# Both halves of the last batch's mix behind the branch to the general path

## The chip, the cores and the metric

One core of a Trainium2 chip runs the kernel. Its engines are TensorE (PE; PEld is its weight load), VectorE (DVE), ScalarE (ACT), GpSimd (POOL) and SyncE (SP), each with its own queue of instructions, released by semaphores. The metric is the device time of one execution in microseconds, median of 3 runs.

## The reference

Four batches of 6208 steps by 256 channels. A gated scan runs along the steps of each batch; then the 128 steps with the highest score (a dot product with `w_gate`) go through a small two-layer network and are mixed back into their rows of the output:

```python
f = lower_bound + (1 - lower_bound) * sigmoid(f_logit);  i = 1 - f
for t in range(S):
    h = f[:, t] * h + i[:, t] * x[:, t];  y[:, t] = h
scores = y @ w_gate
for b in range(B):
    top = argpartition(-scores[b], 128)[:128]
    xe = y[b, top]
    ye = relu(xe @ w1) @ w2                      # 256 -> 1024 -> 256
    out[b, top] = y[b, top] + sigmoid(scores[b, top])[:, None] * ye
```

## The kernel before, in words

The steps are cut into 29 units (`UNITS`), 7 or 8 per batch. For each unit SP loads `ft` and `xt`; ACT makes the gates, POOL and DVE the inputs, DVE scans, PE takes scores and turns the tiles, ACT (and DVE for some) copies them to `ym`, and SP stores them to `out`. After a batch's last unit `choose(b)` finds its 128 rows with a fast search (`idx` and `aim`, the row numbers), and counts in `tally` (DVE, line 480) whether that search could be trusted.

Then `experts(b)` works on these rows: POOL fetches them from `out` (indirect DMA, line 529) into `xe`; PE turns them, and ACT and DVE copy them to `xT`; DVE takes the gate's product (`ask`, line 559), ACT its sigmoid (`opened`, line 563); PE multiplies by `w1` (`up`, 570 or 579), ACT applies the relu (587), PE multiplies by `w2` (`down`, 592 or 597) into PSUM; DVE mixes the product with the row (`mix`, 601 or 604) into `res`; POOL scatters `res` back to `out` (indirect DMA, line 608).

For the last batch, b = 3, `down` and `mix` are cut into two halves of 128 channels (`down_half`, `mix_half`). Both halves of `down` write the one PSUM tile `acc`, columns 0 to 127 and 128 to 255; each is 8 products, which the trace shows as 16 records, so 32 on line 597 in all. `mix_half` is

```python
v.scalar_tensor_tensor(st["res"][:, c], st["py"][:, c], st["open"], st["xe"][:, c], ALU.mult, ALU.add)
```

The **general path** is for inputs on which the fast search fails in some batch. It is an unrolled exact search for all batches (some 7,200 instructions in POOL's queue, few in the others'), and stands behind a branch:

```python
def redo_all():
    v.tensor_reduce(total, tally[:1], AX.X, ALU.add)                    # line 716, DVE
    val = nc.values_load(total[0:1, 0:1], engines=ENGINES)             # line 717: POOL, PE, ACT, DVE
    with tc.If(val != 0):                                              # line 718
        for b in range(B):
            redo(b)
```

DVE adds up `tally`; then POOL, PE, ACT and DVE each load the sum into a register (TENSOR_LOAD) and each branch on it (COMPARE_BRANCH). With these inputs the sum is zero and every engine jumps over the general path to the join behind it. On POOL, the join and the last scatter are all that is left.

The order in each engine's queue comes from a planner, the class `Plan`: each step is put in with `add(engine, cost, emit, rank, after, key)`; the planner simulates the engines with these costs, takes among ready steps the one with the lowest rank, and emits the code in the order of its start times. `after` are the keys that must have been started in its simulation before a step is. Semaphore waits are then derived from the order of emission: a write into `acc` that is emitted after a read of `acc` waits for it, whichever columns they use. The branch is the step `("redo",)`, emitted after the last `down` of batch 3. Line 790 is the end of the program, where the engines meet.

Of the kernel before, what the change touches and what calls it, by code (L numbers as in the profile page):

```python
# [22 lines left out]
NF = F // P  # L23
# [36 lines left out]
class Plan:  # L60
# [6 lines left out]
    def add(self, engine, cost, emit, rank, after, key=None, late=0.0, takes=(), load=1.0):  # L67
        if key is not None:
            self.at[key] = len(self.ops)
        self.ops.append((engine, cost, emit, rank, [k for k in after if k is not None], late, takes, load * cost))  # L70
# [110 lines left out]
def gated_scan_moe(tc, xin, fin, lbwg, w1, w2, outs, cap):  # L181
    nc = tc.nc
    v, a, pe, g = nc.vector, nc.scalar, nc.tensor, nc.gpsimd
    with ExitStack() as ctx:
# [57 lines left out]
        add = plan.add  # L242
# [371 lines left out]
        def experts(b):  # L614
            st = {}
            fetch, turn_in, take, ask, opened, up, relu, down, mix, scatter = stages(b, st)
            turn_half, take_half, up_half, down_half, mix_half, copy_indices, see = st["half"]
            halved = b == B - 1
            p0 = 20.0 * last_unit[b] + EXPERT[b]
            k = lambda *t: ("moe", b, *t)  # L620

            prev = ("mix", b - 1)
            if halved:
                add("pool", 0.15, copy_indices, p0, [("st", b)], ("index", b))
                for i in range(last_unit[b - 1] + 1, N - 1):
                    add("pool", 0.1, lambda i=i: see(i), p0, [("store", i), ("index", b), ("seen", i - 1)], ("seen", i))
            add("pool", 1.04, fetch, p0, [("st", b), ("index", b), ("seen", N - 2) if halved else None, ("store", last_unit[b])], k("fetch"))
            add("sw", 0.36, None, p0 - 1e3, [k("fetch")], k("xe"), late=LAND[b])
            plan.tile(("pm", b, 0), ("pt", "pt"), [("xT", b)])
            if halved:  # L630
                plan.tile(("pm", b, -1), ("pt", "pt"), [("xT", b, 1)])
                for h in range(NH):
                    add("pe", 0.18, lambda h=h: turn_half(h), p0 - 2, [k("xe"), ("moe", b - 1, "down", NF - 1), k("flip", h - 1)], k("flip", h), takes=[("pm", b, -h)])
                    add("dve" if h else "act", 0.28, lambda h=h: take_half(h), p0 - 2, [k("flip", h)], ("xT", b, h) if h else ("xT", b))
            else:
                add("pe", 0.36, turn_in, p0, [k("xe"), ("moe", b - 1, "down", NF - 1)], k("flip"), takes=[("pm", b, 0)])
                add("act", 0.38, take, p0 - 1, [k("flip")], ("xT", b))
            if b in ASKED:
                add("dve", 0.6, ask, p0, [k("xe"), prev, ("wgrow",)], k("ask"))
            else:  # L640
                add("pe", 0.3, ask, p0 - 1, [("xT", b), prev], k("ask"), load=0.1)
            add("act", 0.22, opened, p0 - 1, [k("ask")], k("open"))
            for f0 in range(0, NF, TP) if halved else ():
                for h in range(NH):
                    add("pe", 0.95, lambda f0=f0, h=h: up_half(f0, h), p0, [("xT", b, h) if h else ("xT", b), k("up", f0 - 1), k("uph", f0) if h else None],
                        k("up", f0 + TP - 1) if h else k("uph", f0), takes=[("pm", b, 1 + f0 // TP)])
            for f in range(0 if halved else NF):
                add("pe", 0.49, lambda f=f: up(f), p0, [("xT", b), k("up", f - 1)], k("up", f), takes=[("pm", b, 1 + f // TP)] if f % TP == 0 else [])
            for f0 in range(0, NF, TP):
                plan.tile(("pm", b, 1 + f0 // TP), ("pt", "pt"), [k("relu", f0)])  # L650
                add("act", 0.6, lambda f0=f0: relu(f0), p0 - 1, [k("up", f0 + TP - 1)], k("relu", f0))
            for h in range(NH if halved else 0):
                for f in range(NF):
                    add("pe", 0.24, lambda f=f, h=h: down_half(f, h), p0, [k("relu", f // TP * TP), k("up", NF - 1), k("downh", NF - 1) if h else None, k("down" if h else "downh", f - 1), k("ask"), ("flag", b)],
                        k("down" if h else "downh", f), load=1.0)
            for f in range(0 if halved else NF):
                add("pe", 0.46, lambda f=f: down(f), p0, [k("relu", f // TP * TP), k("up", NF - 1), k("down", f - 1), k("ask"), None if b in APART else ("flag", b),
                                                         ("forget", N - 1, 1) if b in APART else None], k("down", f), takes=[("py", b)] if b in APART else [], load=1.5)
            if b in APART:
                plan.tile(("py", b), ("gt", "gt"), [("mix", b)])  # L660
            if halved:
                add("dve", 0.33, lambda: mix_half(0), p0 - 1, [k("downh", NF - 1), k("open")], k("mixh"))
                add("dve", 0.33, lambda: mix_half(1), p0 - 1, [("redo",), k("mixh"), k("open")], ("mix", b))
            else:
                add("dve", 0.5, mix, p0 - 1, [k("down", NF - 1), k("open")], ("mix", b))
            add("pool", 1.04, scatter, p0, [("mix", b), ("flag", b), ("moe", B - 1, "fetch")], k("scatter"))
            add("sw", 0.36, None, p0 - 1e3, [k("scatter")], ("scatter", b), late=DONE)
# [88 lines left out]
        for b in range(B):  # L756
            choose(b)
            experts(b)
# [35 lines left out]
```

## Time and profile before

| | |
|---|---|
| runs | 212.99 us median of 3 (212.47 to 213.47) |
| the profiled execution | 212.7 us, of which the span from first to last instruction is 210.3 us |
| busy, share of the span | PE 74%, PEld 48%, DVE 75%, ACT 74%, POOL 76% |
| HBM | 53.48 MB read, 25.95 MB written, 378 GB/s over the span |
| granted TensorE clock | 0.905 over the span, 1.00 from 190 to 205 us |
| DMA share, 190 to 195 us; 195 to 200; 200 to 205; 205 to 210 | 0.17; 0.13; 0.02; 0.08 |

The page cuts the span into 40 slices of 5.26 us and gives the busy share of each engine, and of the core's 16 DMA engines, in tenths. The timeline lists instructions in order of time with their idle time before and what released them. The views of a line list its instructions, and those of an engine's sequencer with a q behind the engine's name (POOLq, DVEq, PEldq). The chain that ended last is followed back from the last instruction.

### The profile page before, as it was taken

Reading aid. Unit: us, or ns where it says so; the run is one execution under the profiler, and the core shown is the slowest. Engines: PE = TensorE matmul, PEld = TensorE weight load, DVE = VectorE, ACT = ScalarE, POOL = GpSimd, SP = SyncE. Lnnn points to the kernel's source line nnn. Section 1 sums busy time; section 2 is a strip of 40 time slices with the busy share of each in tenths; the row PEclk is TensorE's granted clock in tenths of the full one; section 3 lists DMA queues with packets and bytes.
Section 4 is the critical chain, followed back from the end, with each engine's and each line's share of the span. In section 5 each row is a group of like instructions: output and inputs, shape, how many; then the busy total and the mean of one; then the engine's idle time right before and its main releaser. Section 6 shows DMA issues by size and latency. Waiting matters only on the chain. (4 is left out here: it accounts for less than half of the span.)

```text
span 210.3 us, 3398 instructions
## 1 busy us (share of the span) xinstructions
PE 155.4 (74%) x1191; PEld 101.9 (48%) x1191; DVE 157.5 (75%) x200; ACT 155.6 (74%) x210; POOL 159.7 (76%) x162
## 2 busy tenths in 40 slices
PE   0775636677779576773878999895699899999950
PEld 0233424444345444431436786462397556467950
DVE  2389599998799998868598979998795988650110
ACT  4698989989869899799868969777988956241300
POOL 5389999784989999987999896597999997024301
PEclk9999999999655999998558999979599999999997
DMA  6999999999999999999999999999999999991100
GB/s 219 382 428 427 427 425 417 429 428 418 417 433 425 421 423 424 433 430 424 414 423 435 414 423 434 424 414 426 420 435 421 422 419 420 422 397 61 65 5 30
DMA packets 13684, 79.69 MB, mean 379 GB/s; under 512 B 1760, under 2 KB 2016, under 8 KB 5728
## 3 DMA queue, kind: packets, MB, share of 16 engines
q1 hardware_dynamic: 13136, 78.39, 89.4%
q0 software_dynamic: 384, 1.05, 1.3%
q8 instruction: 11, 0.18, 0.3%
q14 instruction: 9, 0.07, 0.1%
q10 hardware_dynamic: 144, 0.00, 0.0%
HBM read 53.48 MB, written 25.95 MB: 378 GB/s over the span
## 5 line engine op out<-in xcount | busy, mean ns | idle before, releaser
L293 DVE TENSOR_TENSOR_SCAN xt<-gt,xt 128x1024 f32<-128x1024 f32 (+4 forms) x58 | 114.1, 1984 | 18.1 <-POOL xt L283 14.7
L283 POOL TENSOR_TENSOR xt<-xt,ft 128x1024 f32<-128x1024 f32 (+13 forms) x54 | 91.4, 1699 | 6.5 <-ACT ft L271 3.6
L309 PE MATMUL pt<-ident,xt 128*128 128x128 f32 x384 | 69.7, 323 | 5.0 <-ACT ym L326 3.0
L309 PEld LDWEIGHTS pt<-ident,xt 128*128 128x128 f32 x384 | 54.6, 202 | 30.6 <-ACT ym L326 13.8
L302 PE MATMUL score<-xt,wgr 128*32 128x256 f32 (+1 forms) x400 | 42.6, 439 | 35.5 <-DVE xt L293 34.8
L275 ACT ACTIVATE gt<-ft,nl 128x1024 f32<-128x1024 f32 (+4 forms) x58 | 56.9, 984 | 8.6 <-DVE xt L293 7.4
L279 POOL TENSOR_SCALAR xt<-xt,nl 128x1024 f32<-128x1024 f32 (+13 forms) x54 | 46.3, 861 | 15.4 <-DMA xt<-x 13.7
L326 ACT COPY ym<-pt 128x512 f32<-128x512 f32 (+1 forms) x93 | 48.6, 555 | 8.2 <-PE pt L309 7.8
L271 ACT ACTIVATE ft<-ft 128x2048 f32<-128x2048 f32 (+4 forms) x29 | 47.3, 1632 | 9.2 <-DMA ft<-fl 9.2
L302 PEld LDWEIGHTS score<-xt,wgr 128*32 128x32 f32 x400 | 9.7, 115 | 47.0 <-DVE xt L293 35.7
L290 DVE SCALAR_TENSOR_TENSOR xt<-gt,xt 128x640 f32<-128x640 f32 (+10 forms) x22 | 14.1, 641 | 2.4 <-ACT gt L275 2.4
L461 POOL TENSOR_SCALAR hot<-slot,rank 128x128 bf16<-128x128 bf16 x14 | 8.4, 605 | 9.3 <-DVE vals L456 7.6
L579 PE MATMUL pm<-xT,w1t 128*128 128x128 f32 x96 | 12.1, 280 | 0.4 <-ACT xT L550 0.4
L608 POOL DMA_INDIRECT out<-res,aim x4 | 4.0, 1000 | 10.9 <-issue 10.6
L579 PEld LDWEIGHTS pm<-xT,w1t 128*128 128x128 f32 x96 | 11.2, 192 | 1.3 <-ACT xT L550 0.9
L448 DVE TENSOR_SCALAR_CACHE_REDUCE junk<-acc,mine 128x448 bf16<-128x448 f32 x14 | 9.6, 682 | 2.0 <-ACT junks L445 1.3
L587 ACT ACTIVATE hT<-pm 128x512 f32<-128x512 f32 x8 | 4.8, 596 | 6.3 <-PE pm L570 2.6
L326 DVE COPY ym<-pt 128x512 f32<-128x512 f32 (+1 forms) x11 | 6.9, 627 | 2.2 <-PE pt L309 2.2
L592 PE MATMUL acc<-w2t,hT 128*128 128x256 f32 x32 | 7.3, 382 | 0.0
L592 PEld LDWEIGHTS acc<-w2t,hT 128*128 128x128 f32 x32 | 5.9, 190 | 1.1 <-issue 0.4
L601 DVE SCALAR_TENSOR_TENSOR res<-acc,open,xe 128x128 f32<-128x128 f32 x2 | 0.7, 349 | 7.5 <-PE acc L597 7.5
L529 POOL DMA_INDIRECT xe<-out,idx x4 | 4.6, 1143 | 2.0 <-issue 0.8
(99 smaller groups left out, 91.4 us busy)
## 6 DMA issues: line engine op xcount, KB each, us to landing
ft<-fl SPq DMA_DIRECT2D x20, 1024.0 KB, 16.0
xt<-x SPq DMA_DIRECT2D x20, 1024.0 KB, 15.5
out<-ym SPq DMA_DIRECT2D x20, 1024.0 KB, 15.1
ft<-fl SPq DMA_DIRECT2D x3, 832.0 KB, 15.5
xt<-x SPq DMA_DIRECT2D x3, 832.0 KB, 15.5
out<-ym SPq DMA_DIRECT2D x3, 768.0 KB, 17.5
out<-ym SPq DMA_DIRECT2D x5, 256.0 KB, 16.4
ft<-fl SPq DMA_DIRECT2D x4, 256.0 KB, 16.1
```

The source lines that it names most:

```text
L271: a.activation(fs[i], fs[i], ACTF.Sigmoid, scale=-1.0)
L275: a.activation(gs[i, h][:, :n], fs[i][:, h], ACTF.Identity, scale=nl[:, h : h + 1], bias=1.0)
L279: g.tensor_scalar(xs[i][:, h, c0:], xs[i][:, h, c0:], nl[:, h : h + 1], 1.0, ALU.mult, ALU.mult)
L283: g.tensor_tensor(xs[i][:, h, c0:], xs[i][:, h, c0:], fs[i][:, h, c0:], ALU.mult)
L290: v.scalar_tensor_tensor(xs[i][:, h, :c1], gs[i, h][:, :c1], 1.0, xs[i][:, h, :c1], ALU.subtract, ALU.mult)
L293: v.tensor_tensor_scan(xs[i][:, h], gs[i, h][:, :n], xs[i][:, h], carry[h] if blk0 else 0.0, ALU.mult, ALU.subtract)
L302: pe.matmul(score[j * CG : (j + 1) * CG, b % 2, c0:], wgr[:, h, CG - 1 - r : 2 * CG - 1 - r], xs[i][:, h, c + c0 : c + BLK], start=(h == 0 ...
L309: pe.transpose(pts[key][:, q * P : (q + 1) * P], xs[i][:, h, tail + c :: cols], ident)
L326: (v.tensor_copy if eng == "dve" else a.copy)(out, src)
L448: v.tensor_scalar(junk, acc[:, :ROW], st["mine"][:, k : k + 1], None, ALU.is_gt, ALU.add, accum_out=st["rank"][:, k : k + 1])
L579: pe.matmul(st["pm", f // TP][:, c : c + P], w1t[:, h, f * P : (f + 1) * P], st["xT"][:, h], start=(h == 0), stop=(h == NH - 1))
L592: pe.matmul(st["py"][:, :D], st["hT"][:, f], w2t[:, f], start=(f == 0), stop=(f == NF - 1))
```

## The change

One entry in the list of steps that the first half of the last mix must come after: the branch, `("redo",)`.

```diff
             if halved:
-                add("dve", 0.33, lambda: mix_half(0), p0 - 1, [k("downh", NF - 1), k("open")], k("mixh"))
+                add("dve", 0.33, lambda: mix_half(0), p0 - 1, [("redo",), k("downh", NF - 1), k("open")], k("mixh"))
                 add("dve", 0.33, lambda: mix_half(1), p0 - 1, [("redo",), k("mixh"), k("open")], ("mix", b))
```

On DVE, at the end of the program, before (line 601 is the mix of the last batch, 716 the sum of `tally`, 717 and 718 the load of the sum and the branch; lines 559 and 604 behind the branch belong to the general path):

```order
L543 COPY xT_1868<-pm 128x128 [waits PE_49]
L559 SCALAR_TENSOR_TENSOR res,gate<-xe_109,wgrow 128x256 [waits DMASW3_49]
L601 SCALAR_TENSOR_TENSOR res<-acc,open,xe_109 128x128 [waits PE_49,Activation_49]
L716 TENSOR_REDUCE total<-tally 1x1
L717 TENSOR_LOAD total [waits DVE_49]
L718 COMPARE_AND_BRANCH
...
L718 UNCONDITIONAL_BRANCH
L718 UNCONDITIONAL_BRANCH [waits DVE_49]
L601 SCALAR_TENSOR_TENSOR res<-acc,open,xe_109 128x128 [waits PE_49]
L790 UNCONDITIONAL_BRANCH
```

and now:

```order
L543 COPY xT_1868<-pm 128x128 [waits PE_49]
L559 SCALAR_TENSOR_TENSOR res,gate<-xe_109,wgrow 128x256 [waits DMASW3_49]
L716 TENSOR_REDUCE total<-tally 1x1 [waits DVE_49]
L717 TENSOR_LOAD total [waits DVE_49]
L718 COMPARE_AND_BRANCH
...
L718 UNCONDITIONAL_BRANCH
L718 UNCONDITIONAL_BRANCH [waits DVE_49]
L601 SCALAR_TENSOR_TENSOR res<-acc,open,xe_109 128x128 [waits PE_49,Activation_49]
L601 SCALAR_TENSOR_TENSOR res<-acc,open,xe_109 128x128
L790 UNCONDITIONAL_BRANCH
```

The sum of `tally` now stands right behind `ask` (line 559), with no wait for PE ahead of it; both mixes stand behind the join, the first with the waits for PE and ACT, the second with none.

On PE, at the second product of the second half of `down`:

```order
 L597 MATMUL acc<-w2t,hT 128x128 x3
 L597 MATMUL acc<-w2t,hT 128x128 [waits Activation_49]
-L597 MATMUL acc<-w2t,hT 128x128 x4
-L597 MATMUL acc<-w2t,hT 128x128 [waits DVE_49]
-L597 MATMUL acc<-w2t,hT 128x128 x6
+L597 MATMUL acc<-w2t,hT 128x128 x11
 L717 TENSOR_LOAD total [waits DVE_49]
 L718 COMPARE_AND_BRANCH
```

The ninth product is the first of the second half; the tenth waited for DVE (for the first mix, which reads `acc`), and now no product of the second half waits for DVE.

On POOL the order is the same in both. This is its end, ahead of the branch and behind the general path:

```order
L608 DMA out<-res,aim 6208x256 [waits DMASW2_49,DVE_49]
L717 TENSOR_LOAD total [waits DVE_49]
L718 COMPARE_AND_BRANCH
...
L718 ISA [waits Pool_49,DMASW4_49,DMASW5_49,DMASW3_49,DMASW6_49,DMASW2_49,DMASW7_49,DMASW1_49,DMASW0_49]
L718 UNCONDITIONAL_BRANCH
L608 DMA out<-res,aim 6208x256 [waits DMASW6_49,DMASW5_49,DMASW7_49,DMASW3_49,DVE_49]
L790 UNCONDITIONAL_BRANCH
```

POOL's load of the sum follows the scatter of batch 2 and waits for DVE's line 716; the last scatter waits for DVE (the mixes) and for DMAs.

## Rows read from the trace of the kernel before

**Rows 1.** The page's slices: mean busy share of the DMA engines, in tenths.
```profile
DMA  6999999999999999999999999999999999991100
```

**Rows 2.** Timeline, 180 us to the end: start, us, engine, line, what [idle before <-releaser].
```profile
194.16 0.48 DVE L604 SCALAR_TENSOR_TENSOR res<-py,open,xe 128x256 f32<-128x256 f32 x1 [5.17 <-PE py L592]
...
195.44 0.08 DVE L559 DVE_READ_ACCUMULATOR res<-xe,wgrow 128x1 f32 x1
195.50 0.98 POOL L608 DMA_INDIRECT out<-res,aim  x1 [0.30 <-DVE xT L543]
...
198.78 2.23 PE L597 MATMUL acc<-w2t,hT 128*128 128x128 f32 x18
198.98 0.60 ACT L587 ACTIVATE hT<-pm 128x512 f32<-128x512 f32 x1 [1.13 <-PE pm L570]
201.13 0.35 DVE L601 SCALAR_TENSOR_TENSOR res<-acc,open,xe 128x128 f32<-128x128 f32 x1 [5.61 <-PE acc L597]
201.39 0.13 DVE L716 TENSOR_REDUCE total<-tally 1x1 int32<-1x4 f32 x1
...
201.53 1.83 PE L597 MATMUL acc<-w2t,hT 128*128 128x128 f32 x14 [0.52 <-DVE total L716]
203.40 0.35 DVE L601 SCALAR_TENSOR_TENSOR res<-acc,open,xe 128x128 f32<-128x128 f32 x1 [1.87 <-PE acc L597]
206.51 0.98 POOL L608 DMA_INDIRECT out<-res,aim  x1 [10.03 <-issue]
```

**Rows 3.** Line 717, loads of the sum: ns min/median/max, first and last start us.
```profile
L717 POOLq TENSOR_LOAD <-total x1: 513/513/513, 201.6 to 201.6; - x1
...
L717 PEldq TENSOR_LOAD <-total x1: 493/493/493, 201.6 to 201.6; - x1
```

**Rows 4.** Line 718, the branches and what stands at the join.
```profile
L718 POOLq EVENT_SEMAPHORE  x5: 17/43/43, 204.8 to 205.1; - x5
...
L718 POOLq COMPARE_BRANCH  x1: 53/53/53, 202.1 to 202.1; - x1
L718 DVEq COMPARE_BRANCH  x1: 72/72/72, 202.2 to 202.2; - x1
L718 PEldq COMPARE_BRANCH  x1: 3577/3577/3577, 202.2 to 202.2; - x1
...
L718 DVEq EVENT_SEMAPHORE  x1: 21/21/21, 202.4 to 202.4; - x1
L718 POOLq INC_SWDGE_SEM  x1: 328/328/328, 205.2 to 205.2; - x1
L718 PEldq EVENT_SEMAPHORE  x1: 51/51/51, 205.8 to 205.8; - x1
```

**Rows 5.** DMA queues (packets, MB, share), 195 to 201.5 us; then 203 to 204.2.
```profile
q0 software_dynamic: 96, 0.26, 10.0%
...
q8 instruction: 1, 0.02, 6.0%
q14 instruction: 1, 0.01, 2.2%
```

**Rows 6.** The chain that ended last: start us, us, what.
```profile
204.77 0.09 issue
...
205.76 0.53 issue
206.29 1.21 POOLq L790
```

**Rows 7.** Line 790, the program's end, 204.5 to 206.4 us.
```profile
L790 PEldq DRAIN  x1: 8/8/8, 206.0 to 206.0; - x1
L790 POOLq DRAIN  x1: 2994/2994/2994, 206.3 to 206.3; - x1
```

**Rows 8.** Timeline again: POOL's fetch for batch 3, released by a transfer.
```profile
190.64 0.09 POOL L516 MEMSET ym<- 1x1 f32 x1 [2.32 <-DMA out<-ym]
191.45 1.11 POOL L529 DMA_INDIRECT xe<-out,idx  x1 [0.72 <-DMA out<-ym]
```

## The prediction

> **What bounds the kernel now.** I read the page's slices first: the DMA engines are at 90% or more up to the 36th of 40 slices, so up to about 190 us the kernel is a stream of loads and stores, and behind that it is a chain of small steps for the last batch [rows 1]. The change sits in that chain, so the second view is the timeline from 180 us on. The third is the chain that ended last, and the fourth the two lines of the branch, since the timeline leaves out what sequencers do.
>
> The timeline shows DVE's half of the story [rows 2]. The first mix starts at 201.13 us, 5.61 us after DVE's last step, once PE has done the first half of `down` and one product more. The sum of `tally` comes behind it, at 201.39, although it reads nothing that the mix writes: it is late only because it stands behind the mix in DVE's queue. PE sat idle for 0.52 us until DVE was through and went on at 201.53. The row names line 716 as the releaser, but by the order it is the mix that ends at 201.48 (PE writes `acc`, which the mix reads). PE's last product ends at 201.53 + 1.83 = 203.36, the second mix runs from 203.40 to 203.75, and the last scatter starts on POOL at 206.51, 2.76 us after `res` was whole.
>
> Those 2.76 us are the matter. The four engines load the sum at 201.6, in about 0.5 us [rows 3]. POOL branches at 202.1, in 53 ns, and then shows nothing until its first event at the join at 204.77 [rows 4, 6]: 204.77 - 202.15 = 2.62 us. In that gap the DMA queues carry one packet on each of the two instruction queues, where 195 to 201.5 us had only those of the software queue [rows 5]. I read it as POOL, which jumps over some 7,200 instructions, waiting for the code at its target. PE shows the same as a branch of 3577 ns; DVE is at its join 0.2 us after its branch [rows 4]. At 205.76 POOL is through the join, 3.61 us after its branch, and 0.75 us later the scatter starts [rows 6, 2]. So what ends last is: first mix, sum, load, branch, code, join, scatter. The second mix, at 203.75, is not on that path.
>
> **The change, step by step.**
>
> *The sum and the branch go forward.* The sum now follows `ask`, whose last record ends at 195.52 [rows 2]. With 0.13 us for itself it is done by about 195.7, instead of 201.52. POOL stands behind the scatter of batch 2, which ends at 196.48 [rows 2]. Whether its sequencer takes the load while that scatter runs, or behind it, no row tells: with 0.1 us to start and 0.51 us [rows 3], the branch ends between 196.4 and 197.2. Adding the 3.61 us from branch to the end of the join, POOL stands ready at the last scatter's wait between 200.0 and 200.8, over 2.5 us ahead of the mixes. Load, code and join thus cost nothing; what hides them is the second half of PE's work, and if the code took 2.5 us longer they would show again. The one transfer that the join may have to wait for, batch 2's scatter, is no later than before.
>
> *PE's wait goes.* No product of the second half waits for DVE now. 0.52 us go, and PE's last product ends at 203.36 - 0.52 = 202.84. Its input from ACT is done at 198.98 + 0.60 = 199.58, well before the fifth product needs to follow [rows 2], so nothing else is late there.
>
> *Both mixes come behind the last product.* The first starts 0.12 us after PE (201.01 to 201.13) or 0.04 us (203.36 to 203.40), by the two rows there are [rows 2]; the two take 0.35 us each, back to back. `res` is whole at 202.84 + 0.04 to 0.12 + 0.70 = 203.58 to 203.66; I take 203.62. That is 0.13 us earlier than 203.75: one mix more behind PE costs 0.35, the wait gives 0.52 back. DVE itself waits in the branch from 195.7 to about 196.6, when nothing else is queued for it.
>
> *The scatter now starts from `res`.* How long POOL takes from a release to its start I bound by three rows. The fetch of batch 3 started 0.72 us after the last small step ahead of it (190.73 to 191.45) [rows 8]; the last scatter itself 0.75 us after the join [rows 6, 2]; the scatter of batch 2 0.86 us after its mix ended at 194.64 [rows 2], where it also stood behind another scatter, so this is an upper bound. I take 0.79: 203.62 + 0.79 = 204.41, and 206.51 - 204.41 = 2.10 us are gained. The ends are 203.58 + 0.72 and 203.66 + 0.86, that is 2.21 and 1.99 us.
>
> *The end moves along.* From the scatter's start to the end of the span are 210.3 - 206.51 = 3.8 us: descriptors, landing and the engines' meeting, in which POOL's drain takes up 2.99 us, from 206.29 to 209.28 [rows 7]. Its cover is PE: PE came to the end at 206.0 [rows 7]. If PE reaches the load only when its products are done, it is there at 202.84 + 0.49 + 3.58 + 0.2 = 207.1, and POOL's drain would end at 209.28 - 2.10 = 207.18. So PE is in time even then, by little.
>
> Sum: 212.7 - 2.1 = 210.6 us against the profiled execution. That one is 0.29 us below the median of the runs, so I expect a median of 212.99 - 2.1 = **210.9 us**, 1.0% less.
>
> **A rule against it.** POOL's gap begins at its branch and holds a code packet [rows 4, 5], and I price that branch at 2.62 us. The Trainium skill (Advanced Engine Details and Errata, Control Flow Timing) gives about 108 ns for a compare-and-branch, by which an early branch would be worth next to nothing and only the mixes' 0.13 us would be left. The same skill (Runtime: NRT & Kernel Launch, Instruction fetch mechanics) says that a taken branch whose target is outside the two loaded pages waits for a DMA fetch. The rows bear out the first for POOL's and DVE's own records (53 and 72 ns), and the second for what follows on POOL and PE.
>
> **The rivals.**
>
> *No gain.* POOL's join is late for a cause other than its branch, one that stays, for instance that it follows `res`: 204.77 is 1.02 us after the second mix ended. Then only `res` moves, by 0.13 us, and the time is 212.9. For it: the profile names no releaser for that stretch, only "issue". Against it: by the order the join waits for POOL and DMAs and not for DVE, and the code packets. 8%.
>
> *Slower: the first mix is released by PE's join.* Standing behind the branch, it could be held until PE too has passed, whose event there came at 205.8, 3.58 us after its branch began [rows 4]. If PE takes the load only behind its last product, the join is at 202.84 + 0.1 + 0.49 + 3.58 = 207.0, `res` at 207.7, the scatter at 208.5: 2.0 us later, 215.0 us. If it takes the load as soon as its products are queued, near 199.7, the join is at 203.9 and it would still be a gain of 1.1 us. It decides at 206.51 - 0.79 - 0.70 = 205.0: a later join makes the kernel slower, which is a PE branch that begins after 201.4. Against it: the second mix stood behind the same join before and started 0.04 us after PE's last product, 2.4 us before PE's event. 5%.
>
> *More.* POOL has long been waiting when `res` comes, and starts as soon after it as one scatter follows another, 0.30 us [rows 2]: 203.92, a gain of 2.6 us, 210.4. For it: its sequencer has nothing left to do. Against it: the fetch of batch 3, whose sequencer had also waited, took 0.72. 10%, and within the range.
>
> **The numbers.** The forecast with its own ends has 77%, more gain 10%, no gain 8%, slower 5%. The run-to-run spread of the kernel before (212.47 to 213.47) is the largest part of the range: 210.4 less 0.3 is 210.1; 210.9 plus 0.1 for the ends plus 0.5 for the spread, and 0.3 for a code load that shows again in part, is 211.8. Of changes in time about 0.5%, or 1.07 us, can be told from none, so faster means under 211.93 us. That gives faster 86% (77 and 10, less 1 for a median that the spread lifts over the bound), the same 9%, slower 5%.
>
> **What would show it.** Right: the sum on line 716 near 195.6 us, POOL's branch near 197 and its join over by 201, a code packet near 198; line 597 on PE in one run of 32 records without idle time, ending near 202.8; the two mixes back to back from about 202.9; the last scatter near 204.4, released by DVE and not by "issue". Wrong: a last scatter that still starts over 2 us after the second mix, with events of POOL's join between them; a first mix that starts well behind PE's last product; or a PE that comes to the end after POOL's drain, which would take back part of the gain at line 790.

## The result and the profile after

The changed kernel takes 210.74 us in the median of 6 runs (209.70 to 211.79), the kernel before 213.0 us (212.47 to 214.10). The ratio is 0.9887 with a 95% interval of 0.9842 to 0.9932: faster by 1.4 to 3.4 us. A second measurement gave 0.9916 (0.9884 to 0.9948; 211.99 us median of 10 runs against 213.39). One run in the table of experiments, 212.78 us of the kernel "bank and order", counts as a slow run and is left out of that kernel's median, range and ratio. The profiled execution of the change took 209.75 us, its span 207.4 us.

The timeline of the changed kernel from 195 us on (start, us, engine, line, what, idle before and releaser) answers to [rows 2]:

```profile
195.39 0.08 DVE L559 DVE_READ_ACCUMULATOR res<-xe,wgrow 128x1 f32 x1
195.39 0.14 DVE L716 TENSOR_REDUCE total<-tally 1x1 int32<-1x4 f32 x1
195.43 0.98 POOL L608 DMA_INDIRECT out<-res,aim  x1 [0.30 <-issue]
...
198.72 3.79 PE L597 MATMUL acc<-w2t,hT 128*128 128x128 f32 x32
...
202.64 0.61 DVE L601 SCALAR_TENSOR_TENSOR res<-acc,open,xe 128x128 f32<-128x128 f32 x2 [7.11 <-PE acc L597]
203.52 0.98 POOL L608 DMA_INDIRECT out<-res,aim  x1 [7.11 <-DVE res L601]
```

The sum stands at 195.39 instead of 201.39 us. PE's 32 records are one run without idle time, the two mixes follow it back to back, and the last scatter is released by DVE, no longer by "issue". It starts 2.99 us earlier than before, although the first product on line 597 starts only 0.06 us earlier.

Lines 717 and 718 of the changed kernel (ns min/median/max, first and last start us) answer to [rows 3, 4]:

```profile
L717 POOLq TENSOR_LOAD <-total x1: 512/512/512, 195.6 to 195.6; - x1
...
L717 PEldq TENSOR_LOAD <-total x1: 488/488/488, 200.4 to 200.4; - x1
```
```profile
L718 POOLq EVENT_SEMAPHORE  x5: 17/43/43, 199.2 to 199.5; - x5
L718 POOLq COMPARE_BRANCH  x1: 53/53/53, 196.1 to 196.1; - x1
L718 DVEq COMPARE_BRANCH  x1: 72/72/72, 196.2 to 196.2; - x1
...
L718 PEldq COMPARE_BRANCH  x1: 3717/3717/3717, 201.0 to 201.0; - x1
L718 PEldq EVENT_SEMAPHORE  x1: 51/51/51, 204.7 to 204.7; - x1
```

POOL takes its load at 195.6, while its scatter of batch 2 (195.43 to 196.41) still runs. From its branch to its first event at the join are still 3.05 us (196.15 to 199.20; 2.62 before), but they lie beside PE's products now. The chain that ended last shows POOL's wait as one long piece, where [rows 6] had 0.53 us:

```profile
200.14 0.04 POOLq L608
200.18 3.11 issue
203.29 1.22 POOLq L790
```

From 200.18 POOL waits for `res`. PE is at the join at 204.7, 2 us after the first mix began, so the mixes don't wait for it.

### The profile page after: what moved, and what is told of

Read it like the earlier page. It is cut to its first block, busy times and chain, and to the rows that moved or that the text cites. A ratio compares the mean times of both kernels' runs of the same rounds, so it can differ in the third digit from the quotient of the medians.

```text
span 207.4 us, 3398 instructions
## 1 busy us (share of the span) xinstructions
PE 160.4 (77%) x1191; PEld 103.6 (50%) x1191; DVE 156.8 (76%) x200; ACT 155.6 (75%) x210; POOL 159.8 (77%) x162
## 5 line engine op out<-in xcount | busy, mean ns | idle before, releaser
L309 PE MATMUL pt<-ident,xt 128*128 128x128 f32 x384 | 72.7, 333 | 4.4 <-ACT ym L326 2.9
L309 PEld LDWEIGHTS pt<-ident,xt 128*128 128x128 f32 x384 | 56.3, 204 | 31.6 <-ACT ym L326 14.9
L302 PE MATMUL score<-xt,wgr 128*32 128x256 f32 (+1 forms) x400 | 44.8, 464 | 30.3 <-DVE xt L293 29.6
```

The lines of the kernel that those rows point to most:

```text
L302: pe.matmul(score[j * CG : (j + 1) * CG, b % 2, c0:], wgr[:, h, CG - 1 - r : 2 * CG - 1 - r], xs[i][:, h, c + c0 : c + BLK], start=(h == 0 ...
L309: pe.transpose(pts[key][:, q * P : (q + 1) * P], xs[i][:, h, tail + c :: cols], ident)
```

## The experiments

The path is read from where the edits have not yet acted: from the start of the first product on line 597 to the start of the last scatter. These numbers come from each run's timeline; the last two columns are the runs, and each ratio is to runs of the kernel before in the same series (medians 213.0 to 213.4).

| kernel | first product, us | last scatter, us | path, us | median, us (lowest to highest) | ratio to before, 95% |
|---|---|---|---|---|---|
| before | 198.78 | 206.51 | 7.73 | 213.0 (212.47 to 214.10) | |
| changed | 198.72 | 203.52 | 4.80 | 210.74 (209.70 to 211.79) | 0.9887 (0.9842 to 0.9932) |
| sum early | 199.56 | 204.81 | 5.25 | 210.62 (210.11 to 211.73) | 0.9866 (0.9814 to 0.9918) |
| second bank | 198.66 | 206.38 | 7.72 | 213.00 (212.43 to 213.91) | 0.9982 (0.9959 to 1.0005) |
| short path | 199.58 | 204.83 | 5.25 | 210.21 (209.90 to 210.45) | 0.9838 (0.9802 to 0.9875) |
| no branch | 199.58 | 204.37 | 4.79 | 209.75 (209.36 to 210.16) | 0.9818 (0.9778 to 0.9858) |
| bank and order | 200.80 | 205.26 | 4.46 | 210.07 (209.37 to 211.37) | 0.9835 (0.9791 to 0.9878) |
| whole mix | 199.63 | 204.31 | 4.68 | 211.03 (209.71 to 212.64) | 0.9891 (0.9842 to 0.9940) |
| changed, again | 199.54 | 204.33 | 4.79 | 211.99 (209.73 to 212.62) | 0.9916 (0.9884 to 0.9948) |
| changed, PE short | 199.13 | 203.93 | 4.80 | 209.48 (209.36 to 210.03) | 0.9825 (0.9796 to 0.9855) |
| bank, PE short | 200.47 | 204.93 | 4.46 | 209.62 (209.02 to 210.64) | 0.9824 (0.9791 to 0.9857) |

The start of the first product differs by up to 2.1 us between profiles, and by 0.82 us between two profiles of the same changed kernel, which is why times alone don't settle tenths here, and the path does.

The times also hold what lies outside the span from first to last instruction. That is 2.2 to 2.4 us in every run of the kernels that keep the whole general path, and 1.7 to 1.9 us in all 20 runs of short path, no branch and the two kernels "PE short". So some 0.5 us of the lower medians of these four lie outside everything that the timeline shows, and nothing that happens on the path explains them; what stands there is not shown.

**The sum alone, moved forward.** Mixes, PE's wait and the branch in DVE's order are as before; the step of the branch also comes after the moved sum.

```diff
-        def redo_all():
+        def add_up():
             with nc.allow_low_precision("a sum of four counts"):
                 v.tensor_reduce(total, tally[:1], AX.X, ALU.add)
+
+        def redo_all():
             val = nc.values_load(total[0:1, 0:1], engines=ENGINES)
...
+        add("dve", 0.15, add_up, 20.0 * last_unit[B - 1], [("flag", B - 1)], ("sum",))
```

> The kernel before with one thing moved: the sum of `tally` stands right behind the last entry of `tally` in DVE's order. Both mixes, the branch in DVE's order and PE's wait for the first mix stay as before. Measure: from the start of the first product of line 597 to the start of the last scatter, 206.51 - 198.78 = 7.73 us before and 203.52 - 198.72 = 4.80 us with the change. Theory (the late sum, branch and code load on POOL are what the change takes off the path): POOL's join is over by 201 us, the scatter starts about 0.3 us after the second mix, which ends as before: 203.75 + 0.27 - 198.78 = 5.24 us, so 2.5 us less and a time near 210.5. Rival (PE's removed wait and the mixes' new place make the gain): 7.7 us and a time near 213.

The path is 5.25 us, forecast 5.24. PE and both mixes behave as before, and yet the scatter follows the second mix (timeline of this kernel):

```profile
201.91 0.35 DVE L601 SCALAR_TENSOR_TENSOR res<-acc,open,xe 128x128 f32<-128x128 f32 x1 [5.35 <-PE acc L597]
...
202.32 1.83 PE L597 MATMUL acc<-w2t,hT 128*128 128x128 f32 x14 [0.52 <-DVE res L601]
204.18 0.35 DVE L601 SCALAR_TENSOR_TENSOR res<-acc,open,xe 128x128 f32<-128x128 f32 x1 [1.92 <-PE acc L597]
204.81 0.98 POOL L608 DMA_INDIRECT out<-res,aim  x1 [7.40 <-DVE res L601]
```

So 7.73 - 5.25 = 2.48 of the 2.93 us that the change takes off the path are the early sum; the other 0.45 are PE's wait less the second mix behind it. Here PE's hold is named by its true releaser, the mix (line 601); before, the row named line 716.

**PE's wait alone, removed.** The second half of `down` goes to another PSUM bank, the order stays.

```diff
-                    st["py"] = acc
-                pe.matmul(st["py"][:, h * P : (h + 1) * P],
+                    st["pyh"] = [acc[:, :P], score[:, 1, :P]]
+                pe.matmul(st["pyh"][h],
...
-                v.scalar_tensor_tensor(st["res"][:, c], st["py"][:, c], ...
+                v.scalar_tensor_tensor(st["res"][:, c], st["pyh"][h], ...
```

> The kernel before, with the second half of `down` in the score tile's PSUM bank instead of the columns beside the first half, so that no product waits for the first mix. The order of mixes, sum and branch stays. Theory (late sum and branch): PE is done about 0.8 us earlier, near 202.5, and the second mix near 203.0, but the sum still follows the first mix. That mix no longer waits for the ninth product, so the sum, the branch and the join come some 0.25 us earlier and with them the scatter: 7.5 us from the first product of line 597, a time near 212.8. Rival (PE's wait makes the gain): 4.9 to 5.2 us, a time near 210.5.

The path is 7.72 us (7.5 was expected) and the time the same as before within its interval, though `res` is whole 3.5 us ahead of the scatter (timeline of this kernel):

```profile
200.51 1.95 PE L597 MATMUL score<-w2t,hT 128*128 128x128 f32 x16
200.79 0.35 DVE L601 SCALAR_TENSOR_TENSOR res<-acc,open,xe 128x128 f32<-128x128 f32 x1 [5.12 <-PE acc L597]
201.06 0.13 DVE L716 TENSOR_REDUCE total<-tally 1x1 int32<-1x4 f32 x1
202.50 0.35 DVE L601 SCALAR_TENSOR_TENSOR res<-score,open,xe 128x128 f32<-128x128 f32 x1 [1.31 <-PE score L597]
206.38 0.98 POOL L608 DMA_INDIRECT out<-res,aim  x1 [9.86 <-issue]
```

PE's wait is worth nothing while the branch is late. The sum did come 0.21 us earlier after the first product, as expected, but POOL needed 2.79 us from branch to join here instead of 2.62, and that took it back.

**What POOL does behind its branch.** The order of before, with little to jump over.

```diff
-            for k in range(cap):
+            for k in range(1):
...
             with tc.If(val != 0):
-                for b in range(B):
+                for b in range(1):
```

> The kernel before, its order untouched, with a general path that leaves out three of its four batches and 127 of its 128 rounds of selection (these inputs don't take it), so that POOL jumps over some 30 instructions instead of 7,200. Theory (the 2.62 us behind POOL's branch are the load of the code at its target): no code packet for POOL between branch and join, the join starts within 0.2 us of the branch and is over near 203.3; the scatter follows the second mix: 5.2 us from the first product of line 597, a time near 210.5. Rival (the 2.62 us are the price of any taken branch, or of the join): the join at 204.8 and 7.7 us as before, a time near 213.

The chain that ended last and line 718 of this kernel:

```profile
203.14 0.08 issue
...
203.73 0.86 issue
```
```profile
L718 POOLq COMPARE_BRANCH  x1: 45/45/45, 202.9 to 202.9; - x1
...
L718 PEldq COMPARE_BRANCH  x1: 350/350/350, 203.0 to 203.0; - x1
```

POOL's join begins 0.2 us after its branch and is over at 203.73, and the path is 5.25 us, as with the early sum. PE's branch takes 350 ns instead of 3577. Queue 14, which has a packet behind POOL's branch in every kernel with the long general path, has none here between branch and join. So the 2.62 us [rows 4, 6] are no fixed price of a branch or a join: they depend on how much code is jumped over, and go with the code packet.

**No branch at all.** The changed kernel without the general path.

```diff
-            val = nc.values_load(total[0:1, 0:1], engines=ENGINES)
-            with tc.If(val != 0):
-                for b in range(B):
-                    redo(b)
```

> The changed kernel with the general path left out altogether: no loads of the sum, no branch, no join (the sum itself stays). Theory (with the change, all of it is hidden behind PE's products): the same 4.80 us from the first product of line 597 to the scatter, within 0.1, and the time of the changed kernel, near 210.7, within the spread. Rival (the branch still costs: PE's branch of 3.7 us, POOL's join or the long wait): a scatter over 0.3 us earlier, or an end of the program that comes earlier after the scatter than 207.4 - 203.52 = 3.9 us.

The path is the same, 4.79 us: with the change nothing of POOL's branch is left on it. From the scatter to the end of the span are 208.2 - 204.37 = 3.8 us, against 3.9 with the change. But the runs, 209.36 to 210.16, lie lower and closer together than those of the changed kernel. Some 0.5 us of that lie outside the span, as said above; the rest is taken up below.

**What is left on the path.** Two edits of the changed kernel, and the changed kernel itself on the same chip: the second bank again, now with the mixes behind the branch; and one mix of 256 columns in place of two.

```diff
-                add("dve", 0.33, lambda: mix_half(0), p0 - 1, [("redo",), k("downh", NF - 1), k("open")], k("mixh"))
-                add("dve", 0.33, lambda: mix_half(1), p0 - 1, [("redo",), k("mixh"), k("open")], ("mix", b))
+                add("dve", 0.5, mix, p0 - 1, [("redo",), k("down", NF - 1), k("open")], ("mix", b))
```

> The changed kernel, and the second half of `down` in the score tile's PSUM bank, so that the first mix waits for the first half alone and runs beside the second. Theory (after the change the path is PE's products, then what DVE does behind the last one, then the scatter): the last product ends 3.8 us after the first, the second mix starts 0.04 us later and takes 0.35, the scatter follows 0.27 us later: 4.46 us from the first product of line 597 to the last scatter, 0.34 less than the changed kernel's 4.80; a time 0.3 us below it, less than the runs can tell. Rival (something behind the mixes sets the scatter's start): 4.8 us.

> The changed kernel with one mix of 256 columns in place of the two halves, behind the branch. Theory: 0.48 us (the row of batch 2's mix) instead of 0.61, so 4.67 us from the first product of line 597 to the last scatter, 0.13 less; no difference that the runs can tell. Rival: 4.8 us or more.

> The changed kernel once more, on the same chip as the two others: 4.80 us from the first product of line 597 to the last scatter, 0.27 us from the end of the second mix to the scatter, and a ratio to the kernel before near 0.989.

The paths are 4.46, 4.68 and 4.79 us against 4.46, 4.67 and 4.80 forecast: after the change the path is PE's products, DVE's work behind the last of them, and the scatter. The second bank, which did nothing alone, takes 0.34 us off now that the branch is early (timeline of that kernel):

```profile
200.80 2.01 PE L597 MATMUL acc<-w2t,hT 128*128 128x128 f32 x16
202.65 1.95 PE L597 MATMUL score<-w2t,hT 128*128 128x128 f32 x16
...
204.64 0.35 DVE L601 SCALAR_TENSOR_TENSOR res<-score,open,xe 128x128 f32<-128x128 f32 x1 [1.36 <-PE score L597]
205.26 0.98 POOL L608 DMA_INDIRECT out<-res,aim  x1 [6.61 <-DVE res L601]
```

The times of the three don't measure such tenths. The interval of the whole mix overlaps with both others; those of the second bank and of the changed kernel just miss each other (0.9878 and 0.9884), but their medians are 1.9 us apart, over five times the 0.34 us of path. The third run, the changed kernel unaltered, has a span that is 2.3 us longer than in its first profile. 0.8 of that is there at the first product; the rest comes behind the scatter. Its DMA queues (packets, MB, share), first from 205.4 to 206.6 us, then from 206.6 to 208.5, and its last scatter (us from issue to landing):

```profile
q0 software_dynamic: 45, 0.12, 25.3%
q8 instruction: 1, 0.02, 7.2%
...
q0 software_dynamic: 3, 0.01, 2.4%
...
out<-res,aim POOLq DMA_INDIRECT x1, 4.0
```

and POOL's drain at the end of the program, in this kernel and in the first profile of the change:

```profile
L790 POOLq DRAIN  x3: 40/112/4586, 204.1 to 209.5; - x3
```
```profile
L790 POOLq DRAIN  x3: 40/112/3039, 203.3 to 207.1; - x3
```

A code packet of queue 8 is on its way in the stretch in which the scatter's packets go out. 45 of the 48 go beside it, and 3 come only in the next stretch; the scatter lands after 4.0 us instead of 2.4, and the end is 1.5 us later. Queue 8 had two packets from PE's branch on in every kernel in which that branch took over 3 us, one where it took 0.35 us, and none without a branch. In the first profile of the change its second packet was just behind the scatter's, and the 48 went together:

```profile
q0 software_dynamic: 48, 0.13, 54.7%
q8 instruction: 1, 0.02, 9.7%
```

That first profile has a meeting of the same kind earlier, which the last scatter does not feel. The scatter of batch 2 sends 45 of its 48 packets before 197.55 us, and the other 3 come in the next stretch, beside POOL's code packet on queue 14; it lands after 3.3 us, where it took 2.4 before. From 197.55 to 198.5 us:

```profile
q0 software_dynamic: 3, 0.01, 2.7%
q14 instruction: 1, 0.01, 2.1%
```

**PE's code taken away.** To see whether this meeting sets the changed kernel's spread, the general path keeps POOL's part and loses most of PE's; once on the changed kernel, once with the second bank.

```diff
             fetch()
+            if b:
+                return
             turn_in()
```

> The changed kernel with a general path that leaves out the expert step (PE's, ACT's and DVE's part) of three of its four batches; POOL's part, which is what POOL jumps over, keeps its length. Observed in the second profile of the changed kernel: PE's second code packet was on its way when the packets of the last scatter came, three of these followed only when it was through, and the scatter landed 4.0 us after its issue instead of 2.4. Theory (the code that PE loads behind its branch now meets the last scatter, and how they fall sets part of the spread of the changed kernel's times): PE's branch takes about 0.35 us instead of 3.3 to 3.7, no code packet after about 204 us, the scatter lands 2.4 us after its issue, 4.8 us from the first product of line 597 to the scatter as with the change, and the runs lie closer together, near those without a branch (209.4 to 210.2, against 209.7 to 212.6). Rival (the spread comes from the start of the last batch, elsewhere): times as those of the changed kernel, 210.7 to 212 in the median and up to 212.6.

> The changed kernel with the second half of `down` in the score tile's PSUM bank and with the same shortened general path as the run before this one. Theory: both gains together, 4.46 us from the first product of line 597 to the last scatter, a landing after 2.4 us, and times some 0.3 us below that run. Rival: the times of the run before this one or longer, because the earlier scatter meets PE's code again.

Line 718 stands on line 720 in the first of these; its branches, and its DMA queues from 204 us to the end:

```profile
L720 POOLq COMPARE_BRANCH  x1: 53/53/53, 196.8 to 196.8; - x1
...
L720 PEldq COMPARE_BRANCH  x1: 350/350/350, 201.4 to 201.4; - x1
```
```profile
q0 software_dynamic: 48, 0.13, 5.4%
...
out<-res,aim POOLq DMA_INDIRECT x1, 2.4
```

No code packet is left beside the scatter, the path is 4.80 us as with the change, and the six runs lie within 0.7 us, 209.36 to 210.03, where the changed kernel's lay within 2.1 and 2.9. The median is 1.26 us under that of the changed kernel's first measurement (210.74 - 209.48), which comes from another series. Some 0.5 us of this lie outside the span. In the spans alone the medians are 208.5 us (209.65 in the second measurement) and 207.7, and what of these 0.8 to 2 us is PE's code and what a later first product, the runs don't show. This kernel is no replacement, since its general path is incomplete.

The second one took 0.34 us off the path as forecast, but not off the times: its median is 209.62 us, and its runs, 209.02 to 210.64, lie 1.6 us apart, although PE's code is as short. In its profile the scatter lands after 2.4 us, and the first product starts at 200.47 us, 1.3 us later than in the first one. So PE's code is not needed for a spread of this size, and the narrow one of the first kernel does not show that the meeting makes it. What is shown is the meeting itself and its 1.6 us, in one profile of the changed kernel.

The complete kernel that the experiments point to is the second bank with the mixes behind the branch. Its path is the shortest of the complete ones, 4.46 us, and its ratio 0.9835 (0.9791 to 0.9878); by times it is not told from the first measurement of the change, and only just from the second.

## Why the prediction was right, and where its sizes were off

**What bounded the kernel** was right: the late sum. The early sum alone gave 2.48 of 2.93 us, and the removed wait alone gave nothing.

**The sum and the branch go forward, at no cost** was right. POOL was ready at 200.18, in the forecast stretch of 200.0 to 200.8. The load was taken while the scatter of batch 2 ran, which the prediction had left open. The code took 0.43 us longer than before (3.05 for 2.62), hidden by a slack of over 3 us. That batch 2's scatter would be no later than before was wrong: it started 0.07 us earlier but landed after 3.3 us instead of 2.4, beside POOL's code packet, and that was hidden too. Of the two rules that were set against each other, the short path decides. The Trainium skill's figure for a compare-and-branch (Advanced Engine Details and Errata, Control Flow Timing), about 108 ns, bears on the branch's own record alone, which is shorter still: 45 to 72 ns on POOL and DVE. The Trainium skill's rule that execution goes on only when the code at a far target has been fetched (Runtime: NRT & Kernel Launch, Instruction fetch mechanics) fits what follows: 2.6 to 3.1 us on POOL when 7,200 instructions are jumped over, and 0.2 us when it is some 30.

**PE's wait: 0.52 us** was too small. All of `down` took 2.23 + 0.52 + 1.83 = 4.58 us before and 3.79 now: 0.79. The two pieces beside the hold were longer than their share of the unbroken run, by 0.27 us together; their ends are modelled, so where in them it lay is not shown.

**Mixes behind the last product** were right: the first starts 0.13 us after PE's last product (198.72 + 3.79 = 202.51), and the two take 0.61 us, not 0.70, since they overlap a little.

**POOL's 0.79 us from release to start** was the term most off: it is 0.27 (203.25 to 203.52), and 0.27 to 0.28 in every run whose scatter was released by DVE. The rows taken as bounds were of another kind: POOL had just come through the join, or a transfer had released it. That was the rival "more", at 10%: the scatter that has long been queued starts as soon after its release as one scatter follows another [rows 2].

Together these give 4.80 us of path where the prediction's numbers gave 204.41 - 198.78 = 5.63: 0.27 from PE, 0.04 from the mixes, 0.52 from POOL.

**The end moves along** was the step that failed the other way. The prediction asked only whether PE would come to the end in time (it does, at 204.9, over 1 us ahead of POOL's drain). It did not ask which transfers PE's branch starts, and what they meet. Before, PE's second code packet had been over before the last scatter's packets came; in the two profiles of the change both fall between 205 and 207 us, and in the one in which the code was first, the landing took 1.6 us more.

**That 210.9 us came so close to 210.74 is luck.** The profiled execution, which met no code, took 209.75 us where the working gave 210.6: the working was 0.85 us too slow, and the path above accounts for 0.83 of that. The median lies 1 us above that execution, whose span is among the two shortest of the six (207.3 to 209.5 us). A later first product (up to 2.1 us between profiles) or the meeting with the code (1.6 us) can each do that, and the forecast had neither; which of them it was in which run is not shown.

**The rivals.** "No gain" and "slower" are gone: the join follows POOL's branch and not `res`, and the mixes started at 202.64, 2 us ahead of PE's event at the join.

**What stays open.** Only one profile shows PE's code meeting the last scatter, so how many runs have it is not known. With PE's code short, the median is 3.6 us under the kernel before (213.05 - 209.48), 0.6 more than the path explains; 0.5 of that lie outside the span (2.3 us before, 1.8 here), and why is not known. Why the first product starts up to 2.1 us later in some profiles was not tried. Nor was a complete general path that is short on PE.

## What to carry to other kernels

A branch on data is only as early as its condition in the order of the engine that computes it: put the condition where its inputs are ready, not behind work that it does not need, and work that is still to be done can hide the jump's code load. A wait taken off one engine is worth nothing until the engine that is last has been brought forward, so try parts singly and together. When a chain's end moves, look at what each engine's jump starts on the DMA engines at that moment.

## What the runs showed of the hardware

A jump over the whole general path cost 2.6 to 3.1 us on POOL (some 7,200 instructions) and 3.3 to 3.7 us on PE, with packets on the instruction queues, and 0.2 and 0.35 us where little was jumped over. Twice packets of the kernel's own transfers came late beside such a packet: 3 of the 48 packets of a scatter came after 207 us where the other 45 were over by 206.4, and its landing took 4.0 us instead of 2.4; in the other case 3 of 48 came late, and the landing took 3.3 us. An indirect DMA that has long been queued started 0.27 to 0.28 us after its release; one whose sequencer has just arrived there started 0.75 us later [rows 6, 2]. POOL's sequencer loaded a register (195.6 us) while its own indirect DMA was running (195.43 to 196.41). The time outside the span was 1.7 to 1.9 us in the kernels with a short or no general path on PE, and 2.2 to 2.4 us in all others.
